# Attention and a feed-forward block on one core: the bias sums in four row groups, the first two pairs' bias by products of their own, and the order of loads and weights

## The chip, the core and the metric

The kernel runs on one core of a Trainium2 chip. The core has a matrix engine (TensorE, PE in the profile), a vector engine (VectorE, DVE), an activation engine (ScalarE, ACT), a general engine (GpSimd, POOL) and an engine that here only issues transfers (SyncE, SP). Each works through its own list of instructions in program order and waits on semaphores where it needs another engine's result. ScalarE, GpSimd and SyncE each have a queue for DMA transfers; an issue that has to wait holds up everything behind it on the same engine. The metric is the time of one execution on the device in microseconds, the median over runs.

## The reference

Eight batches of eight heads, 576 positions, head size 64. With `cum` the running sum of `max(s, 0)` along the positions of one head:

```python
scores = scale * np.matmul(q, k.transpose(0, 1, 3, 2))
bias = -(cum[:, :, :, None] - cum[:, :, None, :])
scores = np.where(causal, -1000000000.0, scores + np.minimum(bias, 0.0))
attn = softmax(scores)
x = (attn @ v), heads side by side: 4608 tokens x 512
h = x @ w_in                      # 512 x 2048
g = h * np.clip(h + 3.0, 0.0, 6.0) / 6.0
out = g @ w_out                   # 2048 x 512, float32
```

## The kernel before

**Pairs.** The 64 heads are worked in 32 pairs `p`, four pairs (`PPB`) to a batch. For each pair q and k are loaded (`load_qk`, 288 KB each), cast to f16 (`cast_qk`, a tile `tok`), transposed into a tile `qk` with head size on partitions 0 to 63 (`transpose`, `order`), and v is loaded and cast (`load_v`, `cast_v`). There are three buffers each of raw q/k, raw v, `qk` and `va`, so a load waits for the cast three pairs earlier, and the writing of `qk` waits for the scores three pairs earlier. Pairs 0 to 8 are transposed on TensorE; from pair 9 (`NPE`) on a crossbar DMA does it (`crossbar_qk`, issued by SyncE, tile `jt`), and `spread` copies its result into `qk` on VectorE.

**Scores.** `scores(p, hh, g)` makes one 128x512 bank of scores (keys on partitions): `g == 0` holds the four diagonal blocks, `g` 1 and 2 what lies off the diagonal; `corner` makes the last 64 queries of both heads. ScalarE takes the exponential of each bank. `av` multiplies with v, `norm` divides, `transpose_x` (later `crossbar_x`) puts the result into `xT`.

**Bias.** The bias is a product of four rows in partitions 64 to 67 of `qk`, beside the 64 rows of q and k: the query side holds -c, 1, 1, 1, the key side 1 and c in three f16 pieces whose sum is c exactly enough (c is 8 times the running sum). These rows are made for all 64 heads at once on 64 partitions, one head each, in lines 536 to 551: `spos`, the scan `c8`, and then casts and differences on ScalarE and VectorE into `aug`. `load_aug` then moves one head's rows from `aug` to four partitions of `qk` by DMA, issued by SyncE for pairs 0 to 2 and by GpSimd after.

**Causal mask.** In pairs 0 to 3 a product of `ident2` (twice the identity) and `shut` (0 or -65504) is added to the diagonal blocks. From pair 4 on the diagonal blocks contract over all 128 partitions: partitions 68 to 127 hold a fixed staircase (`set_stair`) and VectorE takes the minimum with `masks` after the exponential.

**Feed-forward.** `m1` makes one 128x512 piece of h from four products over `xT` and a slice of `w_in`, then ScalarE and VectorE make `gT`; `m2` multiplies with `w_out`. `group()` picks the next m1 or m2 that is ready when the program is written; before the first m2 only every second call does work, so pairs 4 to 6 hold four m1 each. A block's m1 may begin once its batch has gone through attention, so the first m1 stands in pair 4. The weights come in four pieces of `w_in` and eight of `w_out`, issued by GpSimd (`next_weights`) in the pair loop: none in pair 0, one a pair in 1 to 4, two in 5 and 6, three in 7.

**Order.** The order on each engine is written out by hand; no planner moves it. The loop (line 579) first gives GpSimd and SyncE the work for pairs ahead (aug rows for pair p+2, cast of q and k for p+2, v for p+1, weights, loads for p+3 or p+4), and then the pair's own products, with `get(0)` and `get(1)` where a coming pair's q and k are transposed. Ahead of the loop stand the loads of pairs 0 to 2, the fills, the bias rows and the transposes of pairs 0 and 1.

Of the kernel before, what the change touches and what calls it, by code (L numbers as in the profile page):

```python
# [18 lines left out]
def kernel(  # L19
# [27 lines left out]
    VW = 66  # L47

# [6 lines left out]
    masks_dram = nc.inline_tensor(  # L55
        np.concatenate([tri] * 4 + [tri4] * 2, axis=1).astype(np.float16), name="masks"
# [40 lines left out]
    aug = keep("aug", [NHEADS, 4, 2, SEQ], F16)  # L97
# [41 lines left out]
    def load_aug(p, engs):  # L139
        for hh, eng in enumerate(engs):  # L140
            g = 2 * p + hh
            eng.dma_start(  # L142
                out=qks[p % NQK][64:68, hh, :, 64 * hh : 64 * hh + SEQ],
                in_=aug[g : g + 1, :, :, :],
            )
# [136 lines left out]

    def scores(p, hh, g):
# [3 lines left out]
        by_product = p < PPB  # L287
        if g == 0:
            rows = slice(0, 68 if by_product else 128)
            if by_product:  # L290
                mm(S, lhsT=ident2, rhs=shut[:, 0:512], start=True, stop=False)
            for j in range(4):
# [8 lines left out]
        else:  # L301
            for j in ((0, 3) if g == 1 else (1, 2)):
# [7 lines left out]
                    stop=(c != 0),  # L310
                )
        c = slice(512 * g, 512 * (g + 1))
# [6 lines left out]
    def corner(p):  # L319
        S = s_bank([128, 2, 64], "Sc")  # L320
        by_product = p < PPB
# [9 lines left out]
        for hh in range(2):  # L331
            qT, kT = qk_of(p, hh)
            mm(  # L333
# [86 lines left out]
    def m1(n, ft):  # L420
        if ft == 0:
            gTs[n] = work.tile([128, NFT, 512], F16, tag="gT", bufs=2, name="gT")
        ph = psum.tile([128, 512], F32, tag="ph", bufs=2, name="ph")
        for kc in range(NKC):
# [6 lines left out]
            )  # L431
        tr = work.tile([128, 512], F32, tag="tr", bufs=3, name="tr")
# [64 lines left out]
    s_all = work.tile([NHEADS, SEQ], F32, tag="s_all", bufs=1)  # L497
    nc.sync.dma_start(out=s_all, in_=s.rearrange("b h t -> (b h) t"))
    nc.scalar.dma_start(out=stair_sb, in_=stair_dram.ap())
    load_qk(0, 0, nc.sync)  # L500
    load_qk(0, 1, nc.scalar)
    nc.scalar.dma_start(out=ident, in_=ident_dram.ap())
    nc.scalar.dma_start(out=masks, in_=masks_dram.ap())
# [3 lines left out]
    load_v(0, nc.sync)  # L507

# [9 lines left out]
    fill(nc.gpsimd, aug[:, 0, 1, :], 1.0)  # L518
    fill(nc.gpsimd, aug[:, 1:4, 0, :], 1.0)
    for i in range(NQK):  # L520
        init_va(i, nc.gpsimd)
    ones = work.tile([NHEADS, SEQ], F32, tag="ones", bufs=1)
    nc.vector.memset(ones, 1.0)
    nc.vector.memset(bias3, 3.0)
    for i in range(NQK):
        for hh in range(2):
            r = SEQ + 64 * hh
            nc.vector.memset(qks[i][0:64, hh, :, r : r + 64], 0.0)
    for t in Ps:
        fill(nc.vector, t[:, 1536:1664], 1.0)  # L530
    for t in PCs:
        fill(nc.vector, t[:, 128:192], 1.0)
    set_stair(0, nc.gpsimd.tensor_copy)
    set_stair(1, nc.gpsimd.tensor_copy)

    spos = work.tile([NHEADS, SEQ], F32, tag="spos", bufs=1)
    nc.vector.tensor_scalar(
        out=spos, in0=s_all, scalar1=0.0, scalar2=8.0, op0=ALU.max, op1=ALU.mult
    )
    c8 = work.tile([NHEADS, SEQ], F32, tag="c8", bufs=1)  # L540
    nc.vector.tensor_tensor_scan(
        out=c8, data0=ones, data1=spos, initial=0.0, op0=ALU.mult, op1=ALU.add
    )
    nc.scalar.mul(out=aug[:, 0, 0, :], in_=c8, mul=-1.0)
    nc.vector.tensor_copy(out=aug[:, 1, 1, :], in_=c8)
    r1 = work.tile([NHEADS, SEQ], F32, tag="s_all", bufs=1, name="r1")
    nc.vector.tensor_tensor(out=r1, in0=c8, in1=aug[:, 1, 1, :], op=ALU.subtract)
    nc.vector.tensor_copy(out=aug[:, 2, 1, :], in_=r1)
    nc.vector.tensor_tensor(
        out=aug[:, 3, 1, :], in0=r1, in1=aug[:, 2, 1, :], op=ALU.subtract  # L550
    )

    cast_qk(0, nc.scalar.copy, nc.scalar.copy)
    load_aug(0, (nc.sync, nc.sync))
    for i in range(2):
        load_qk(2, i, nc.sync)
# [151 lines left out]
```

## Time and profile before

| | |
|---|---|
| median of 13 runs | 374.43 us (372.36 to 377.52) |
| profiled execution | 374.06 us |
| its span | 372.3 us |
| TensorE busy | 347.0 us (93%) |
| VectorE busy | 242.8 us (65%) |
| ScalarE busy | 219.5 us (59%) |
| GpSimd busy | 118.7 us (32%) |

A line of the timeline or of the POOL order has its start in us, its length, the engine, the line of the kernel, the operation, what is written and read, the shape, how many were merged, and in brackets the idle time before it and what ended it. A line of the waits names the waiting engine and line, what it waited for, and the sum in us, the number of times and the longest. In the stretches each engine's busy time stands with its number of instructions (PE, PEld, DVE, ACT, POOL), then the granted TensorE clock, the DMA share and GB/s. A matmul's length is until its result is there; back to back they follow each other faster than that. Pair `p`'s first product in the trace is at 15.28 us for p = 0, 21.53, 27.32 and 30.76 for 1 to 3, 38.48 for 4, 46.42, 53.96, 61.20, 71.00 and 80.72 for 5 to 9.

### The profile page before, as it was taken

What the parts mean: (1) busy time and instruction counts of PE and PEld (TensorE: products, weight loads), DVE (VectorE), ACT (ScalarE), POOL (GpSimd) and SP (SyncE); (2) the same over time, 40 slices, a digit from 0 to 9 for tenths busy, and PEclk for the clock granted to TensorE, in tenths of its full rate; (3) what the DMA queues carried; (4) which work ended last, traced back from release to release, by engine and by line L of the source; (5) the groups of instructions that cost most, each with busy time, mean ns of one, the idle gap of its engine ahead of it and who ended that gap; (6) DMA issues with size and microseconds to landing.
All of it is one profiled execution on the core that took longest, in us unless ns stands there. A gap on an engine that the chain in (4) does not pass through costs nothing.

```text
span 372.3 us, 7613 instructions
## 1 busy us (share of the span) xinstructions
PE 347.0 (93%) x2845; PEld 193.3 (52%) x2845; DVE 242.8 (65%) x541; ACT 219.5 (59%) x384; POOL 118.7 (32%) x214
## 2 busy tenths in 40 slices
PE   1597999879999899999999999999999999999995
PEld 0376666445555455555555555555555444444442
DVE  6655799567778977777777777777775554544531
ACT  3456798646667566666666666666666334344310
POOL 9373949543335233333333333333300000000000
PEclk9999799989999999999999999999999999999999
DMA  9579999999989999899989999998311010010012
GB/s 188 110 148 223 225 238 218 202 206 215 209 178 176 218 185 172 183 178 178 178 152 204 178 171 185 177 180 150 81 48 46 30 55 30 30 56 29 30 56 85
DMA packets 158189, 54.01 MB, mean 145 GB/s; under 512 B 146928, under 2 KB 153248, under 8 KB 158152
## 3 DMA queue, kind: packets, MB, share of 16 engines
q1 hardware_dynamic: 150408, 48.23, 65.7%
q0 software_dynamic: 6144, 4.74, 7.7%
q10 hardware_dynamic: 1600, 0.56, 0.7%
q8 instruction: 22, 0.36, 0.4%
q14 instruction: 15, 0.12, 0.1%
HBM read 37.11 MB, written 9.44 MB: 125 GB/s over the span
## 4 chain that ended last, share of the span: by engine, by line
PE 76%; DMA 10%; SPq 5%; POOL 4%; DVE 2%; issue 2%; ACT 0%; POOLq 0%
PE po L445 32%; PE ph L425 29%; PE O L362 6%; PE S L305 5%; DMA raw<-in_q_dram 5%; DMA vraw<-in_v_dram 3%; PE S L294 3%; DMA jt<-tok 2%; SPq L130 1%; SPq L134 1%; SPq L119 1%; POOL tok L194 1%; POOL tok L190 1%; POOL qk L142 1%; DVE qk L226 1%
## 5 line engine op out<-in xcount | busy, mean ns | idle before, releaser
L434 DVE SCALAR_TENSOR_TENSOR gT<-tr,ph 128x512 f16<-128x512 f32 x144 | 98.6, 685 | 89.8 <-ACT tr L433 89.1
L425 PE MATMUL ph<-xT,w_in_sb 128*128 128x512 f16 x576 | 149.3, 382 | 0.3 <-DVE gT L434 0.3
L433 ACT ACTIVATE tr<-ph,bias 128x512 f32<-128x512 f32 x144 | 99.0, 687 | 82.8 <-PE ph L425 71.8
L445 PE MATMUL po<-w_out_sb,gT 128*128 128x512 f16 x576 | 145.6, 379 | 1.3 <-DVE x L385 1.3
L313 ACT ACTIVATE P<-S 128x512 f16<-128x512 f32 x192 | 112.0, 595 | 41.9 <-PE S L294 20.9
L445 PEld LDWEIGHTS <-gT 128*128 128x128 f16 x576 | 50.3, 98 | 47.6 <-DVE x L385 1.4
L425 PEld LDWEIGHTS <-w_in_sb 128*128 128x128 f16 x576 | 51.5, 98 | 44.6 <-issue 1.5
L142 POOL DMA_DIRECT2D qk<-aug x58 | 34.0, 587 | 122.1 <-PE Sc L333 58.3
L362 PE MATMUL O<-va,P 128*128 128x65 f16 x896 | 49.6, 197 | 4.3 <-POOL va L202 2.2
L305 PE MATMUL S<-qk 68*128 68x448 f16 (+3 forms) x256 | 50.8, 284 | 0.2 <-ACT P L313 0.2
L362 PEld LDWEIGHTS <-P 128*128 128x128 f16 x896 | 41.3, 100 | 17.6 <-DVE x L385 2.4
L305 PEld LDWEIGHTS <-qk 68*128 68x128 f16 x256 | 24.6, 102 | 24.7 <-issue 1.4
L194 POOL CAST tok<-raw 128x576 f16<-128x576 f32 x51 | 32.7, 673 | 8.2 <-DMA raw<-in_q_dram 6.5
L226 DVE COPY qk<-jt 64x768 f16<-64x768 f16 x92 | 31.7, 344 | 3.5 <-DMA jt<-tok 2.1
L385 DVE TENSOR_TENSOR x<-O,rl 128x320 f16<-128x320 f32 x64 | 31.5, 492 | 2.2
L454 DVE TENSOR_SCALAR ob<-po 128x512 f32<-128x512 f32 x36 | 24.6, 682 | 9.5 <-PE po L445 9.5
L294 PEld LDWEIGHTS <-qk 128*128 128x128 f16 (+1 forms) x256 | 20.3, 101 | 16.2 <-issue 2.6
L315 DVE TENSOR_TENSOR P<-P,masks_sb 128x512 f16<-128x512 f16 x56 | 24.7, 440 | 4.8 <-ACT P L313 4.8
L294 PE MATMUL S<-qk 128*128 128x128 f16 (+1 forms) x256 | 26.1, 226 | 1.5 <-DVE qk L226 0.9
L202 POOL CAST va<-vraw 128x512 f16<-128x512 f32 x32 | 19.9, 623 | 4.4 <-DMA vraw<-in_v_dram 2.5
L240 PE MATMUL pt<-ident,tok 128*128 128x128 f16 (+1 forms) x40 | 6.1, 288 | 12.1 <-ACT tok L194 8.2
L384 DVE RECIPROCAL rl<-O 128x5 f32<-128x5 f32 x64 | 12.1, 189 | 6.5 <-PE O L362 6.5
(49 smaller groups left out, 151.5 us busy)
## 6 DMA issues: line engine op xcount, KB each, us to landing
raw<-in_q_dram SPq DMA_DIRECT2D x32, 288.0 KB, 6.3
out_dram<-ob SPq DMA_DIRECT2D x36, 256.0 KB, 2.2
raw<-in_k_dram SPq DMA_DIRECT2D x31, 288.0 KB, 7.2
vraw<-in_v_dram SPq DMA_DIRECT2D x64, 128.0 KB, 4.4
w_in_sb<-in_moe_w_in_dram POOLq DMA_DIRECT2D x4, 512.0 KB, 9.5
w_out_sb<-in_moe_w_out_dram POOLq DMA_DIRECT2D x8, 256.0 KB, 6.6
vraw<-in_v_dram SPq DMA_DIRECT2D x32, 32.0 KB, 3.4
qk<-aug POOLq DMA_DIRECT2D x58, 9.0 KB, 3.5
```

Source lines behind the costliest of these rows:

```text
L142: eng.dma_start(out=qks[p % NQK][64:68, hh, :, 64 * hh : 64 * hh + SEQ], in_=aug[g : g + 1, :, :, :],)
L194: eng(out=tok[:, 9 * D * i : 9 * D * (i + 1)], in_=raws[p % NRAW][:, 9 * D * i : 9 * D * (i + 1)],)
L226: copies[par](out=qk[0:64, :, i, 128 * par : 128 * par + 256 * n].rearrange("p h (s two c) -> p h s two c", two=2, c=128)[:, :, :, 0, :], ...
L294: mm(S[:, c], lhsT=kT[rows, c], rhs=qT[rows, c], start=(j == 0 and not by_product), stop=(j == 3),)
L305: mm(S[:, c : c + w], lhsT=kT[0:68, 128 * j : 128 * (j + 1)], rhs=qT[0:68, 128 * (j + 1) : SEQ], start=(c == 0), stop=(c != 0),)
L313: nc.scalar.activation(out=pt[:, c], in_=S, func=AF.Exp, scale=0.125)
L362: mm(o[:, i, :], lhsT=lhsT, rhs=va[:, hh, j, 0:65], **kw)
L385: nc.vector.tensor_tensor(out=X[p][:, :, hh, :], in0=o[:, :, 0:64], in1=rl.to_broadcast([128, 5, 64]), op=ALU.mult,)
L425: mm(ph, lhsT=w_in_sb[:, kc, ft * 128 : (ft + 1) * 128], rhs=xT[:, kc, n * 512 : (n + 1) * 512], start=(kc == 0), stop=(kc == NKC - 1),)
L433: nc.scalar.activation(out=tr, in_=ph, func=AF.Relu, bias=bias3[:, 0:1])
L434: nc.vector.scalar_tensor_tensor(out=gTs[n][:, ft, :], in0=tr, scalar=6.0, in1=ph, op0=ALU.min, op1=ALU.mult)
L445: mm(po, lhsT=gTs[n][:, ft, t4 * 128 : (t4 + 1) * 128], rhs=w_out_sb[:, ft, :], start=(ft == 0), stop=(ft == NFT - 1),)
```

## The change

**Bias rows.** s is loaded for 32 heads at a time, four copies on 128 partitions, so each head has four partitions (32 apart). `rows_of[n]` holds the query side and the key side of all four rows. It is made by `cum1` to `cum6`: for heads 0 to 31 ahead of the loop, mostly on VectorE, and for heads 32 to 63 in pairs 6 to 11, mostly on GpSimd with the scan on VectorE. `load_aug` reads `rows_of`.

**Pairs 0 and 1.** They have no `load_aug`. Rows 64 to 67 of their `qk` are zero, and their bias is added by products over all 128 partitions of `rows_of` with `picked`, a copy of the query side in which `sel` leaves only one head's four partitions: nine more products a head.

**Queues.** SyncE issues no `load_aug` any more; pair 2's goes to GpSimd. Pair 0 to 2's loads go out ahead of everything that waits for a result; `load_v(p + 3)` moves to the top of the loop. ScalarE's queue has two pieces of s, k of pair 0, ident, shut, and stair last. Pair 1's casts go to GpSimd.

**Masks and stairs.** `shut` is loaded instead of `masks`; GpSimd makes `masks` in pair 4. Pair 4 now uses the product with `shut` too. The staircases are set on GpSimd in pairs 4 and 5 (six copies), none ahead of the loop. Pair 5's `load_aug` moves from pair 3 to pair 4.

**Order.** Each of pairs 0 to 7 transposes the next pair, in pairs 0 to 3 after the second bank and before head 1. Weights: one piece in pairs 2 and 3, three in 4, four in 5, three in 6. In pair 4 two m1 begin with three of their four products (`m1_begin`), ahead of the last head's `av` and after the second bank.

```diff
-    aug = keep("aug", [NHEADS, 4, 2, SEQ], F16)
+    rows_of = keep("rows_of", [128, 2, 640], F16, 2)
+    sel = keep("sel", [128, 4], F32)
+    picked = keep("picked", [128, 4, SEQ], F16)
...
+    def by_rows(p, hh, out, keys, queries):
+        mm(
+            out,
+            lhsT=rows_of[0][:, 1, keys],
+            rhs=picked[:, 2 * p + hh, queries],
+            start=False,
+            stop=False,
+        )
...
-        by_product = p < PPB
+        by_product = p <= PPB
...
+            if p < NROW:
+                for j in range(4):
+                    c = slice(128 * j, 128 * (j + 1))
+                    by_rows(p, hh, S[:, c], c, c)
...
+            if p < NROW:
+                for j in ((0, 3) if g == 1 else (1, 2)):
+                    c = OFF[j] - 512 * g
+                    w = 448 - 128 * j
+                    mm(
+                        S[:, c : c + w],
+                        lhsT=rows_of[0][:, 1, 128 * j : 128 * (j + 1)],
+                        rhs=picked[:, 2 * p + hh, 128 * (j + 1) : SEQ],
+                        start=False,
+                        stop=(c != 0),
+                    )
...
+    def m1_begin(n, ft, kcs):
+        if (n, ft) not in phs:
+            ph = psum.tile([128, 512], F32, tag="ph", bufs=2, name="ph")
+            phs[n, ft] = [ph, 0]
+        ph, have = phs[n, ft]
+        for kc in range(have, kcs):
...
-    s_all = work.tile([NHEADS, SEQ], F32, tag="s_all", bufs=1)
-    nc.sync.dma_start(out=s_all, in_=s.rearrange("b h t -> (b h) t"))
+    def load_s(n, engs):
+        C[n] = work.tile([128, SEQ], F32, tag="s_all", bufs=1, name="s_all")
+        heads = s.rearrange("b h t -> (b h) t")[32 * n : 32 * (n + 1), :]
+        for r, eng in enumerate(engs):
+            eng.dma_start(out=C[n][32 * r : 32 * (r + 1)], in_=heads)
+
+    load_s(0, (nc.sync, nc.scalar, nc.sync, nc.scalar))
+    load_qk(0, 1, nc.scalar)
+    load_qk(0, 0, nc.sync)
+    nc.scalar.dma_start(out=ident, in_=ident_dram.ap())
+    nc.scalar.dma_start(out=shut, in_=shut_dram.ap())
     nc.scalar.dma_start(out=stair_sb, in_=stair_dram.ap())
...
+    for i in range(2):
+        load_qk(2, i, nc.sync)
+    load_v(1, nc.sync)
...
+    fill(nc.gpsimd, rows_of[0][:, 0, :], 1.0)
+    fill(nc.gpsimd, rows_of[0][:, 1, SEQ:640], 0.0)
+    for i in range(NROW):
+        fill(nc.gpsimd, qks[i][64:68, :, :, :], 0.0)
...
-    set_stair(0, nc.gpsimd.tensor_copy)
-    set_stair(1, nc.gpsimd.tensor_copy)
...
+    nc.vector.tensor_reduce(
+        out=sel,
+        in_=ident.rearrange("p (r g) -> p g r", r=4)[:, 0:4, :],
+        axis=mybir.AxisListType.X,
+        op=ALU.add,
+    )
+    nc.vector.tensor_scalar_mul(out=ident2, in0=ident, scalar1=2.0)
...
+    V = nc.vector
+    cum1(0, V)
+    cum2(0)
     cast_qk(0, nc.scalar.copy, nc.scalar.copy)
-    load_aug(0, (nc.sync, nc.sync))
...
+    nc.scalar.copy(out=rows_of[0][0:32, 0, 0:SEQ], in_=C["c"][0:32])
     for i in range(2):
         load_qk(3, i, nc.sync)
     load_v(2, nc.sync)
+    cum3(0, V)
+    cum4(0, V)
+    cum5(0, V)
+    cum6(0, V)
+    pick(0)
+    transpose(0, 0, (nc.scalar.copy, nc.vector.tensor_copy))
+    transpose(0, 1, (nc.scalar.copy, nc.scalar.copy))
+    for g in range(1, 2 * NROW):
+        pick(g)
+    cast_qk(1, nc.gpsimd.tensor_copy, nc.gpsimd.tensor_copy)
+    for i in range(2):
+        load_qk(4, i, nc.sync)
     cast_v(0)
+    load_aug(2, nc.gpsimd)
...
+    weights_in = {2: 1, 3: 1, 4: 3, 5: 4}
     for p in range(NP):
         nxt = p + 1 < NP
-        if 0 < p < NP - 2:
-            load_aug(p + 2, (nc.gpsimd, nc.gpsimd))
-        c = 3 if p == 0 else p + 2
-        if p != 1 and c < NP:
+        if p + 3 < NP:
+            load_v(p + 3, nc.sync)
+        if p == 4:
+            set_stair(2, nc.gpsimd.tensor_copy)
+            load_aug(5, nc.gpsimd)
+            set_stair(0, nc.gpsimd.tensor_copy)
+            nc.gpsimd.tensor_scalar(
+                out=masks, in0=shut, scalar1=65504.0, scalar2=None, op0=ALU.add
+            )
+        if p == 5:
+            set_stair(1, nc.gpsimd.tensor_copy)
+        if 0 < p < NP - 2 and p != 3:
+            load_aug(p + 2, nc.gpsimd)
+        c = p + 2
+        if p and c < NP:
             cast_qk(c, nc.gpsimd.tensor_copy, nc.gpsimd.tensor_copy)
...
-        next_weights(0 if p < 1 else 1 if p < 5 else 2 if p < 7 else 3)
+        next_weights(weights_in.get(p, 3 if p > 2 else 0))
...
+        if p == 6:
+            load_s(1, (nc.sync,) * 4)
+            fill(nc.gpsimd, rows_of[1][:, 0, :], 1.0)
+        if p == 8:
+            cum1(1, nc.gpsimd)
+        if p == 9:
+            cum2(1)
+            nc.gpsimd.tensor_copy(out=rows_of[1][0:32, 0, 0:SEQ], in_=C["c"][0:32])
+        if p == 10:
+            cum3(1, nc.gpsimd)
+            cum4(1, nc.gpsimd)
+        if p == 11:
+            cum5(1, nc.gpsimd)
+            cum6(1, nc.gpsimd)
...
             scores(p, 0, 1)
+            get(0)
             scores(p, 0, 2)
...
+            get(1)
             scores(p, 1, 0)
             scores(p, 1, 1)
-            get(0)
...
         if p == PPB:
+            early[0] = False
+            scores(p, 0, 0)
             av(p - 1, 1, 0)
+            m1_begin(0, 0, NKC - 1)
             av(p - 1, 1, 1)
             norm(p - 1, 1)
-            scores(p, 0, 0)
             scores(p, 0, 1)
+            m1_begin(0, 1, NKC - 1)
             transpose_x(p - 1)
-            early[0] = False
+            group()
+            group()
             scores(p, 0, 2)
             get(0)
-            group()
-            group()
```

## The prediction

> **What bounds it now.** First the page, part 2: TensorE is busy in tenths 9 nearly throughout, except in the first nine slices of 9.3 us. So the end is set by TensorE, and only gaps and slow clock near the start can be won.
>
> ```profile
> PE   1597999879999899999999999999999999999995
> ...
> PEclk9999799989999999999999999999999999999999
> ```
>
> Then the stretches of 5 us:
>
> ```profile
> 10.00:15.00 5.00, 1.29 (x9) 0.82 (x9) 4.89 (x10) 1.24 (x2) 1.88 (x3) 1.00 0.03 6
> 15.00:20.00 5.00, 4.94 (x35) 3.23 (x35) 0.99 (x3) 4.16 (x8) 1.76 (x3) 1.00 0.97 188
> ...
> 35.00:40.00 5.00, 4.14 (x50) 3.58 (x50) 1.93 (x6) 2.54 (x5) 4.99 (x9) 0.54 1.18 218
> ...
> 75.00:80.00 5.00, 3.57 (x27) 2.31 (x28) 2.81 (x9) 0.89 (x3) 0.66 (x2) 0.66 1.47 217
> ```
>
> From 10 to 15 us nothing loads (6 GB/s) and VectorE works 4.89 of 5 us; at 35 and 75 us the granted clock drops. The waits, Sync's queue first, name the causes: the bias rows hold Sync 3.7 us; v is cast late; the crossbar's jt lands late.
>
> ```profile
> SPq L142 <- DVE aug L549: 3.7, 1, 3.7
> ```
> ```profile
> PE O L362 <- POOL va L202: 2.2, 1, 2.2
> ...
> DVE qk L226 <- DMA jt<-tok: 2.1, 1, 2.1
> ```
>
> The timeline gives the prices: S by ident2 and shut took 0.61 us at 15.28 and 0.39 at 27.32.
>
> ```profile
> 2.98 6.36 POOL L511 COPY qk<-stair_sb 64x1280 f16<-64x1280 f16 x4
> ...
> 8.26 1.68 DVE L547 TENSOR_TENSOR r<-c,aug 64x576 f32<-64x576 f32 x1
> ...
> 15.28 0.61 PE L291 MATMUL S<-shut,ident 128*128 128x512 f16 x1
> ...
> 15.69 0.63 PE L294 MATMUL S<-qk 68*128 68x128 f16 x4
> ```
> ```profile
> 27.32 0.39 PE L291 MATMUL S<-shut,ident 128*128 128x512 f16 x1
> ...
> 27.55 0.39 PE L294 MATMUL S<-qk 68*128 68x128 f16 x4
> ```
> ```profile
> 26.81 1.16 POOL L142 DMA_DIRECT2D qk<-aug  x2
> 30.19 0.82 POOL L190 CAST tok<-raw 96x768 f16<-96x768 f32 x1 [2.22 <-DMA raw<-in_q_dram]
> 34.43 0.82 POOL L190 CAST tok<-raw 96x768 f16<-96x768 f32 x1 [3.42 <-DMA raw<-in_k_dram]
> 35.20 0.61 POOL L202 CAST va<-vraw 128x512 f16<-128x512 f32 x1
> ```
>
> **Bias chain.** The sum c was ready at 6.86 (4.57 + 2.29). Now VectorE first takes sel and ident2 from ident, which stands behind two s pieces (148 KB) and k on ScalarE's queue. Masks, next behind ident, landed 5.8 us after issue, at 8.2; ident at about 6.2, plus 1.0 for what is put ahead of it (an estimate, at half of the 225 GB/s of that stretch): 7.2. Then 0.3 for sel and ident2, spos 0.6, scan 2.3 and gaps 0.2: c at 10.6, 3.7 us later. The casts and differences after it took 6.97 to 12.05, 5.1 us, because each ran into a GpSimd copy.
>
> **A rule against the row.** L547 began at 8.26; the last stair copy ended at 9.34; 9.34 + 0.6 is its end, 9.94. The Trainium skill ("SBUF — State Buffer", Who interferes with whom) says why: VectorE and GpSimd share a port pair held for a whole instruction, the other waits. The stairs leave the start, but casts of pair 1 on GpSimd (0.67 each) begin at 11.4, inside the new chain. By undisturbed rows (0.45 + 0.6 + 0.4 + 0.6 + pick 0.35) the rows stand at 13.2; by the rule, one cast between each two steps, at 14.9. I take 14.4, nearer the rule, since L548 and L549 at 9.98 and 10.86 alternated with casts just so.
>
> At nothing, with their cover: GpSimd's fills of rows_of and of qk rows 64 to 68 (0.82 for 864 elements in L174, so 1.45 for each 1536) end by 6, its next work waits for c until 11; without that cover, 3 us. ScalarE's two more issues (0.35 to 0.69 each) and its table load of 1.28 end near 5.3, before q has landed (before, cast at 7.48). The stair load, now last, is first read in pair 4. Picks 1 to 3 (0.35 each) lie under head 0's slow products.
>
> **Products.** Each head of pairs 0 and 1 gains nine products of 1600 columns, 3200 a pair. From L294, (0.63 - 0.31)/3 for 128 columns slow, 0.058 fast: 2.7 us a pair slow, 1.45 fast. Before, S began at 15.28, pair 0 took 6.25 (to 21.53), pair 1 5.79 (to 27.32), pair 2 3.44. After: pair 0 slow is 6.25 + 2.7 = 8.95; pair 1 fast is 3.44 + ten transposes 0.65 + 1.45 = 5.5. Transposing pair 1 inside pair 0 replaces pair 2's transposes, so nothing else changes there.
>
> **The clock, rule and row.** The skill ("TensorE: Matmul & The Clock Gate", Part 1) gives half clock until one busy window of about 3.4 us, free-running. The stretches fit such windows: 0.54 and 0.78 after 35 us mean slow from about 35.4 to 42.2, two windows; 0.66 means one. But from 15.28 TensorE was dense and still took 0.62 for S at 24.27: the PEclk row shows nothing of it. By the rule alone pair 0 would be fast from about 18, by the row only from 24.7. What tells the windows apart is a guess of mine: counting columns at the slow 0.83 ns, those that stayed slow spent 60 to 63% on products other than transposes, those that freed it 65 to 91%. The added products raise pair 0 to about 73%. I take one window earlier, 21.3. Pair 0: 14.4 + 6.9 + 1.05 = 22.4; pair 1 ends at 27.9, its last score 0.55 earlier as before: T = 27.35, against 26.78.
>
> **GpSimd after T.** Its aug load for pair 4 must wait for that last score. Queued behind it, in order, by rows: aug 0.6, two casts 1.65, v 0.9, w_in 0.78; next pair casts 1.65, v 0.9, w_in 0.78; then pair 4: stair 3.2 (two of 1.6), aug 1.2, stair 3.2, masks 0.8, aug 1.2, casts 1.65, v 0.9, three weights 2.3; then pair 5: stair 3.2, aug 1.2, casts 1.65. Sum 27.8, so pair 7's tok is ready at 55.1. Masks has no row; 0.8 is half a stair copy for half its elements, ends 0.3 (VectorE's L565) and 1.5. TensorE used tok 7 at 54.19: it is 0.95 late, and TensorE waits for it: pairs 2 and 3 take 4.0 each (3.44 and five or six transposes twice), so pair 4 begins at 35.9; pairs 4 and 5 take 7.4 each (before, pair 5 began at 46.42, 6 at 53.96, 7 at 61.20) and some 2 for w_in below, so it would ask at about 53.5.
>
> ```profile
> 54.19 0.42 PE L246 MATMUL pt<-ident,tok 96*128 96x96 f16 x6
> ```
>
> So most of what the loads win is handed to this queue. w_in 0, issued at T + 3.15 = 30.5 instead of 26.03, lands in 7.2 to 9.8 (before's least and most): 37.7 to 40.3, asked for at 36.6. That wait of 1 to 3.7 stays under GpSimd's. The other three pieces are wanted one pair each later.
>
> **Loads.** Sync no longer waits for aug, so the 5 idle us carry 1.0 MB and q, k, v of pairs 2 to 4 come about 4 us earlier; that alone removes the 2.2 us wait at 33.4 and the slow 35.4 to 42.2, worth 5 if nothing replaced it. The queue above does. Sync moves past load_v, four s loads (4 x 0.5 us issue, under pairs of 7 us) and no aug.
>
> **jt.** Pair 9's crossbar was issued at 67.29, landed in 7.76; VectorE's spread held norm and TensorE (74.3 to 76.4), then one slow window: about 3 us. After: the cast ends at T + 27.8 + 12.7 = 67.9, and fewer loads stand before it. Median landing over all jt is 6.0: 73.9, wanted near 73 in a program 0.95 late. I take 2.3 of the 3; ends 0 and 3.5.
>
> **The rest.** Pair 4 by product: 1152 columns, 0.5 us, hidden under GpSimd's wait; without that cover, +0.5. It saves three VectorE minima. The products begun early fill a gap, no more work. Pairs 8 to 11 get the second sum: a 2.3 us scan on VectorE, and GpSimd steps of about 0.7 to 1.5 (estimates from its casts, doubled for two inputs). VectorE has 20 to 30% free there; L315 took 1.36 instead of 0.42 at 116.99 beside a cast. I add 0.4, ends 0 and 1.5.
>
> **Sum.** +0.95 - 2.3 + 0.4 = -0.95. Profiled execution: 374.06 with a span of 372.3, 1.76 around it; so 373.1. The median shown is 374.43, 0.37 above, so 373.5.
>
> **Rivals.** *Early clock* (0.30): the gate opens at 17.9. Pair 0 ends at 20.7, T is 25.65, pair 7's tok 0.75 early; jt saves the whole 3.5, 0.2 lost later: 370.4. For it: the products' density; against: 9 us of slow, dense work before.
>
> *GpSimd's queue is the bound, slower* (0.26): the gate opens at 24.7 as before. Then T is 29.0, tok 7 is 2.6 late, jt is late with it and saves nothing, 0.5 later: 377.5. It decides from T above 28.3, where lateness 1.9 plus 0.4 eats the 2.3. For it: 9.6 us of stair copies that before lay at 2.98 to 9.34, under the loads; against: from 26 to 53 us GpSimd lost 10.7 us to waits for DMA (2.22 and 3.42 of them above), which the earlier loads take away.
>
> *Hidden anyway* (0.10): the start does not move since ident and port waits put the rows at 15.3 and loads are again held by casts: 374.4.
>
> **Numbers.** Sum case 0.34, rest as given. The measurement tells about 0.5% from nothing, 372.6 to 376.3. Faster: the early clock's 0.30 and 0.09 of the sum's case; slower: 0.26 and 0.02; same 0.33. Range 369.2 to 378.2, from the early clock less 1.2 (weights and jt at best) to the queue's case plus 0.7; the sum's own range, 371.5 to 375.6, from the ends of jt and masks.
>
> **What would show it.** First S near 14.4; S products of 0.39 from about 21; loads busy from 10 to 15; GpSimd without a gap from 27 to 58, and TensorE waiting for tok in pairs 5 or 6; no wait for jt near 74. Wrong if the rows stand before 13 or after 16, if GpSimd's stair copies take other than 1.6, or if VectorE's port waits stall pairs 8 to 11.

## The result: 1.3% slower, where 0.2% faster was forecast

The changed kernel took 379.20 us, the median of 11 runs (377.39 to 379.85), against 374.51 us for the kernel before, measured beside it. The ratio is 1.0126, with a 95% interval of 1.0102 to 1.0149. The forecast was 373.5 us, 0.2% faster, with a range up to 378.2, so both the sign and the range were missed. The profiled execution after took 378.55 us with a span of 376.7; before, 374.06 with 372.3. The difference that has to be found is 4.4 us of span.

The page of the changed kernel, its row of TensorE and its row of the granted clock:

```profile
PE   1598888649999899999999999999999999999995
...
PEclk9999999959999999999999999999999999999999
```

Each digit is 9.4 us. The slow clock of the fifth slice is gone, as the loads were to do, but there is a hole of 4 in the ninth slice, at 75 to 85 us, and the clock there is 0.5. In stretches of 5 us (columns as before: PE, PEld, DVE, ACT, POOL busy, clock, DMA share, GB/s):

```profile
10.00:15.00 5.00, 1.19 (x10) 1.06 (x10) 4.80 (x10) 2.63 (x4) 4.44 (x7) 1.00 1.35 217
...
35.00:40.00 5.00, 3.67 (x45) 2.26 (x43) 1.65 (x5) 2.06 (x4) 4.89 (x6) 1.00 1.18 231
40.00:45.00 5.00, 4.55 (x62) 2.97 (x59) 4.63 (x8) 4.87 (x11) 5.00 (x8) 1.00 0.63 158
45.00:50.00 5.00, 4.44 (x54) 2.82 (x51) 4.92 (x11) 4.79 (x10) 4.95 (x7) 1.00 0.95 134
...
75.00:80.00 5.00, 0.00 (x0) 0.00 (x0) 0.75 (x4) 0.00 (x0) 3.35 (x4) 0.50 0.91 185
```

From 10 to 15 us the DMA engines now carry 217 GB/s instead of 6. From 40 to 50 us they carry 158 and 134, where the kernel before had 235:

```profile
40.00:50.00 10.00, 10.00 (x102) 6.17 (x101) 8.87 (x16) 8.30 (x17) 6.70 (x12) 0.89 1.20 235
```

From 75 to 80 us TensorE of the changed kernel does nothing at all. The waits say what for, first all engines, then Sync's own:

```profile
PE O L394 <- DVE x L417: 8.6, 2, 8.3
...
DVE qk L232 <- DMA jt<-tok: 8.3, 1, 8.3
```
```profile
SPq L134 <- POOL va L209: 11.5, 3, 8.0
```

VectorE's spread of pair 9 (L232) waits 8.3 us for the crossbar's result jt, norm (L417) stands behind it, and TensorE behind norm. Before, the same wait was 2.1. On Sync one load of v waited 8.0 us for a v cast of GpSimd. Its timeline shows what came of that:

```profile
35.78 0.44 SPq L118 DMA_DIRECT2D raw<-in_k_dram  x1
44.23 0.94 SPq L134 DMA_DIRECT2D vraw<-in_v_dram  x2
...
47.82 5.91 SPq L123 DMA_DIRECT2D raw<-in_k_dram  x1
53.83 8.21 SPq L134 DMA_DIRECT2D vraw<-in_v_dram  x2
...
66.51 7.06 SPq L545 DMA_DIRECT2D s_all<-in_s_dram  x4
73.68 1.22 SPq L134 DMA_DIRECT2D vraw<-in_v_dram  x2
...
75.72 1.36 SPq L274 DMA_TRANSPOSE jt<-tok  x1
```

Sync issues nothing from 36.2 to 44.2 us: `load_v(8)`, moved to the top of the loop body of pair 5, waits for `cast_v(5)`, and q and k of pairs 8 and 9 stand behind it. From 48 on single lines of this list take 5 to 8 us, where the kernel before had 3.7 at most:

```profile
54.39 3.71 SPq L130 DMA_DIRECT2D vraw<-in_v_dram  x2
...
67.29 2.43 SPq L268 DMA_TRANSPOSE jt<-tok  x1
```

The crossbar of pair 9 goes out at 75.72 instead of 67.29, though its cast was done at 67.1. Up to 47.8 us Sync is not behind the kernel before: there q of pair 8 was issued at 49.29, here at 45.92. The hold uses up the lead that the early loads had won, and the changed kernel falls behind in the full stretch after it. GpSimd's timeline shows why the v cast came so late:

```profile
32.97 2.45 POOL L563 COPY qk<-stair_sb 64x1280 f16<-64x1280 f16 x2
35.36 1.19 POOL L146 DMA_DIRECT2D qk<-rows_of  x2
36.55 2.45 POOL L563 COPY qk<-stair_sb 64x1280 f16<-64x1280 f16 x2
39.10 1.82 POOL L669 TENSOR_SCALAR masks_sb<-shut 128x640 f16<-128x640 f16 x1
40.89 1.17 POOL L146 DMA_DIRECT2D qk<-rows_of  x2
42.05 1.61 POOL L196 CAST tok<-raw 96x768 f16<-96x768 f32 x2
43.59 0.62 POOL L208 CAST va<-vraw 128x512 f16<-128x512 f32 x1
44.15 0.29 POOL L209 CAST va<-vraw 64x128 f16<-64x128 f32 x1
```

In pair 4 the stairs, the masks, two moves of bias rows and the q/k casts, some 11 us, stand ahead of the cast that Sync waits for.

How the 4.4 us add up is read from the first product of each pair:

| pair | before | after | after minus before |
|---|---|---|---|
| 4 | 38.48 | 34.61 | -3.87 |
| 5 | 46.42 | 44.06 | -2.36 |
| 7 | 61.20 | 58.66 | -2.54 |
| 8 | 71.00 | 68.98 | -2.02 |
| 9 | 80.72 | 84.75 | +4.03 |

The changed program is 3.9 us ahead at pair 4 and still 2.0 at pair 8. Between pair 8 and pair 9 it loses 6.0, the growth of TensorE's wait there from 2.1 to 8.3. From pair 9 to the end it loses another 0.4.

### The profile page after: what moved, and what is told of

Read it like the earlier page. It is cut to its first block, busy times and chain, and to the rows that moved or that the text cites. A ratio compares the mean times of both kernels' runs of the same rounds, so it can differ in the third digit from the quotient of the medians.

```text
span 376.7 us, 7742 instructions
## 1 busy us (share of the span) xinstructions
PE 345.2 (92%) x2884; PEld 191.8 (51%) x2884; DVE 243.8 (65%) x541; ACT 219.3 (58%) x383; POOL 134.2 (36%) x231
## 2 busy tenths in 40 slices
DMA packets 158485, 54.41 MB, mean 144 GB/s; under 512 B 147072, under 2 KB 153344, under 8 KB 158448
## 4 chain that ended last, share of the span: by engine, by line
PE 77%; DVE 7%; DMA 6%; POOL 3%; issue 2%; ACT 2%; ACTq 0%; SPq 0%; POOLq 0%; DVEq 0%
PE po L487 31%; PE ph L460 30%; PE O L394 6%; PE S L324 6%; PE S L313 3%; DMA raw<-in_q_dram 2%; DMA w_in_sb<-in_moe_w_in_dram 2%; DMA ident<-ident_f 2%; DVE gT L476 1%; DVE qk L232 1%; DMA jt<-tok 1%; ACT tr L475 1%; POOL tok L196 1%; DVE x L417 1%; ACT P L343 1%
## 5 line engine op out<-in xcount | busy, mean ns | idle before, releaser
L146 POOL DMA_DIRECT2D qk<-rows_of x60 | 35.4, 590 | 122.4 <-PE Sc L365 52.4
L394 PE MATMUL O<-va,P 128*128 128x65 f16 x896 | 48.2, 193 | 8.6 <-DVE x L417 8.6
L394 PEld LDWEIGHTS <-P 128*128 128x128 f16 x896 | 39.8, 97 | 22.0 <-DVE x L417 9.2
L324 PE MATMUL S<-qk 68*128 68x448 f16 (+3 forms) x256 | 49.8, 276 | 0.2 <-ACT P L343 0.2
L232 DVE COPY qk<-jt 64x768 f16<-64x768 f16 x92 | 34.1, 371 | 9.6 <-DMA jt<-tok 8.3
L200 POOL CAST tok<-raw 128x576 f16<-128x576 f32 x52 | 33.9, 684 | 4.6 <-DMA raw<-in_q_dram 4.1
L417 DVE TENSOR_TENSOR x<-O,rl 128x320 f16<-128x320 f32 x64 | 31.5, 492 | 2.2
L313 PEld LDWEIGHTS <-qk 128*128 128x128 f16 (+1 forms) x256 | 19.5, 98 | 15.7 <-issue 2.4
L313 PE MATMUL S<-qk 128*128 128x128 f16 (+1 forms) x256 | 25.1, 220 | 1.5 <-DVE qk L232 0.9
```

The source lines that it names most:

```text
L146: eng.dma_start(out=qks[p % NQK][64:68, hh, :, 64 * hh : 64 * hh + SEQ], in_=rows_of[g // 32].rearrange("(r g) i t -> g r i t", g=32)[g % ...
L200: eng(out=tok[:, 9 * D * i : 9 * D * (i + 1)], in_=raws[p % NRAW][:, 9 * D * i : 9 * D * (i + 1)],)
L232: copies[par](out=qk[0:64, :, i, 128 * par : 128 * par + 256 * n].rearrange("p h (s two c) -> p h s two c", two=2, c=128)[:, :, :, 0, :], ...
L313: mm(S[:, c], lhsT=kT[rows, c], rhs=qT[rows, c], start=(j == 0 and not by_product), stop=(j == 3),)
L324: mm(S[:, c : c + w], lhsT=kT[0:68, 128 * j : 128 * (j + 1)], rhs=qT[0:68, 128 * (j + 1) : SEQ], start=(c == 0), stop=(c != 0 and p >= NROW),)
L394: mm(o[:, i, :], lhsT=lhsT, rhs=va[:, hh, j, 0:65], **kw)
```

## The experiments

The question was what makes pair 9's crossbar late. At first there were three theories. S: the four loads of s, which stand on Sync ahead of it and took 7.06 us there. D: the DMA engines are full from 50 to 72 us and hold up whatever Sync issues next. G: GpSimd's stairs keep casts and loads back.

Two things hold for all the runs below. Each version was measured beside the kernel before, whose median was then 374.6 to 375.2 us; so versions are compared by their ratios, and 0.1% is 0.37 us. And each trace is of one execution, which need not be a typical one: with the v loads back it took 374.87 us (median 373.09), with four v tiles 375.87 (373.83), with the v loads back and the sum first 373.53 (370.28, and no run was slower).

**The s loads behind the crossbar.**

```diff
-        if p == 6:
+        if p == 7:
             load_s(1, (nc.sync,) * 4)
+        if p == 6:
             fill(nc.gpsimd, rows_of[1][:, 0, :], 1.0)
```

> The changed kernel with the four loads of the second half of s moved from pair 6 to pair 7, behind the crossbar of pair 9 in Sync's queue. Theory S (Sync's order: the four s loads, 7.06 us in the queue from 66.51, hold the crossbar): v of pair 10 starts at 66.5, the crossbar is issued near 69 to 71 instead of 75.72, lands in 3.5 to 5, TensorE's wait of 8.3 us before 80.54 shrinks to 3 or less: 5 us less, about 374. Rival D (the DMA engines are full from 50 to 72 us and hold whatever comes next on Sync): v of pair 10 takes the 5 us in the queue instead, the crossbar is issued at 73 or later, 2.5 us less at most: 376.7 or more.

Measured: 378.13 us, ratio 1.0113 (1.0058 to 1.0167). The time that the s loads had taken on Sync went to the v load behind them; the crossbar went out at 73.29 and TensorE waited 6.1 us. Sync's timeline of this run:

```profile
66.23 5.96 SPq L134 DMA_DIRECT2D vraw<-in_v_dram  x2
...
73.29 1.41 SPq L274 DMA_TRANSPOSE jt<-tok  x1
```

What fills Sync is not s itself but that nothing can be issued quickly then. The four runs do not tell this version from the changed kernel (1.0126). S falls.

**The v loads back behind the q and k loads.**

```diff
-        if p + 3 < NP:
-            load_v(p + 3, nc.sync)
         if p == 4:
...
                     load_qk(m, i, nc.sync)
+        if p + 3 < NP:
+            load_v(p + 3, nc.sync)
         if p == 6:
```

> The changed kernel with the v loads for pair p+3 back behind the crossbar and the q and k loads of the loop, as before the change; the s loads stay in pair 6 ahead of the crossbar. Theory S: the crossbar of pair 9 passes the v loads of pair 10, which stood 2.0 us in Sync's queue, and still waits for the s loads: issue near 73.7, 2 us less, about 377.2. Rival D: the order of v is nothing to a full DMA; 379 and the crossbar's issue near 75.

Measured: 373.09 us, ratio 0.9935 (0.9899 to 0.9971). By the ratios this one edit takes 1.9% (some 7 us) off the changed kernel and makes it faster than the kernel before. That was more than any theory had said. Sync's timeline:

```profile
38.55 0.81 SPq L118 DMA_DIRECT2D raw<-in_q_dram  x1
39.41 0.45 SPq L118 DMA_DIRECT2D raw<-in_k_dram  x1
...
66.06 2.44 SPq L545 DMA_DIRECT2D s_all<-in_s_dram  x4
68.60 1.92 SPq L274 DMA_TRANSPOSE jt<-tok  x1
```

q and k of pair 8 go out at 38.55 instead of 45.92 us, the DMA engines carry 201 GB/s from 40 to 50 us instead of 146, and the crossbar is out 7.1 us earlier; TensorE still waits 3.9 us behind norm at pair 9. A new theory, V, follows: `load_v` at the top of the body waits for a v cast that GpSimd reaches late, and holds q and k of the coming pairs behind it; the DMA engines run half empty meanwhile, are full later, and cannot catch up before pair 9's crossbar.

**Fewer weights early.**

```diff
-    weights_in = {2: 1, 3: 1, 4: 3, 5: 4}
+    weights_in = {2: 1, 3: 1, 4: 2, 5: 2, 6: 2, 7: 3, 8: 1}
```

> The changed kernel with the weight pieces of pairs 4 to 8 spread as 2, 2, 2, 3, 1 instead of 3, 4, 3 in pairs 4 to 6. Sync's order stays. Theory S: Sync's queue still meets the four s loads ahead of the crossbar; 377.5 to 379.5. Rival D: with 0.5 MB of weights less in the DMA queues between 52 and 68 us the s loads take about 3 us instead of 7 in Sync's queue, the crossbar is issued 4 us earlier, 375; and pair 8's aug rows wait less on GpSimd (58.95).

From pair 4 on these are as many pieces, pair by pair, as the kernel before had issued. Measured: 376.87 us, ratio 1.0070 (1.0036 to 1.0105), 0.6% under the changed kernel. The crossbar went out at 70.40. Part of the gain came back as a wait of TensorE for w_out (2.1 us), and its wait behind norm at pair 9 was 2.9. So the earlier weights are a part of the loss and not the larger one, and what is put off is soon wanted.

**The stairs in earlier pairs.**

```diff
+    set_stair(2, nc.gpsimd.tensor_copy)
     load_aug(2, nc.gpsimd)
...
+        if p in (1, 2):
+            set_stair(p - 1, nc.gpsimd.tensor_copy)
         if p == 4:
-            set_stair(2, nc.gpsimd.tensor_copy)
             load_aug(5, nc.gpsimd)
-            set_stair(0, nc.gpsimd.tensor_copy)
...
-        if p == 5:
-            set_stair(1, nc.gpsimd.tensor_copy)
```

> The changed kernel with the six staircase copies taken out of GpSimd's pairs 4 and 5 and set ahead of the bias loads of pairs 2, 3 and 4, where GpSimd waited 0.45, 2.09 and 2.30 us for TensorE. Theory G (GpSimd's 7.3 us of stairs keep casts back, so loads pause at 39 to 45 us and pile up at 50 to 72): pair 4's work on GpSimd starts 2.5 us later than 32.97 but pair 6's and 7's casts 2.5 and 5 us earlier, loads between 40 and 50 above 146 GB/s, the crossbar earlier by 2 or more: 376 to 377. Theory S alone: pair 4's weights come later, nothing else: 379 to 380.

Measured: 379.05 us, ratio 1.0120 (1.0067 to 1.0173). The stairs now delayed the first piece of w_in, for which TensorE waited 6.0 us at 41.2, and Sync still stood until 45.3. The v cast that Sync waits for still ended at 45.5, now because the q and k casts ahead of it waited 2.4 and 0.8 us for their loads. Moving GpSimd's work to another pair only moved the wait; this run neither confirms G nor clears GpSimd.

**Four raw v tiles: the wait taken away, the order kept.** This is the sharpest test of V. The load of v for pair 8 goes into a tile that was free long before.

```diff
-    vraws = keep("vraw", [128, 2, 5, D], F32, NRAW)
+    vraws = keep("vraw", [128, 2, 5, D], F32, 4)
...
-        vraw = vraws[p % NRAW]
+        vraw = vraws[p % 4]
...
-    ones = work.tile([128, SEQ], F32, tag="ones", bufs=1)
-    nc.vector.memset(ones, 1.0)
+    ones = work.tile([128, SEQ], F16, tag="ones", bufs=1)
+    fill(nc.vector, ones, 1.0)
```

> The changed kernel with four raw v tiles instead of three (to make room, the scan's ones are 16-bit), all orders left as they are: load_v of pair 8 now waits for the v cast of pair 4 instead of pair 5's, which is long done. Theory V (that wait, standing ahead of the next pair's q and k loads on Sync, leaves the DMA engines idle at 40-45 us and full to 72): the 8.0 us wait of L134 is gone, q and k of pair 8 are issued at about 38-39 us instead of 45.9, jt at about 68-69, and the time is within 1 us of the run with the v loads put back: 373 us or so, ratio 0.992 to 0.997. Theory D (the order of the bytes in the full stretch decides, the wait is only a bystander): v still goes ahead of q and k, jt stays at 75 or so, 378 to 379 us. Theory G (GpSimd's casts are what is late): unchanged, 378 to 379.

Measured: 373.83 us, ratio 0.9989 (0.9962 to 1.0015): 1.4% (5 us) under the changed kernel, with v still ahead of q and k. Sync's timeline:

```profile
39.83 0.63 SPq L118 DMA_DIRECT2D raw<-in_q_dram  x1
40.51 0.45 SPq L118 DMA_DIRECT2D raw<-in_k_dram  x1
...
67.56 1.36 SPq L274 DMA_TRANSPOSE jt<-tok  x1
```

The crossbar goes out at 67.56, and nothing waits for jt any more. V stands, and D and G in the form that they were given fall. The 16-bit ones, which made room for the fourth tile, changed nothing at the start: the scan took 1.36 us as before and the first product stood at 13.83 (13.95). The ratio is 0.002 (0.7 us) above the range that V gave. In the profile TensorE waited 3.2 us for w_in 0 at 38.7 instead, and its clock was 0.50 from 39.7 to 49.9; six of the 21 runs, of 372.3 to 373.9 us, had a granted clock of 1.00 throughout, so this does not happen in every execution.

**The same edit alone in the kernel before.**

```diff
         nxt = p + 1 < NP
+        if p + 3 < NP:
+            load_v(p + 3, nc.sync)
...
                     load_qk(m, i, nc.sync)
-        if p + 3 < NP:
-            load_v(p + 3, nc.sync)
```

> The kernel before with that one edit alone: load_v(p + 3) at the top of the loop body. Its GpSimd has no stairs and no masks to set in pairs 4 and 5, so the v cast that load_v waits for is early. Theory V (two edits are needed together: the v loads ahead AND the late v cast): within 0.4% of before, jt of pair 9 issued at 67 to 69. A rival (v ahead of q and k is costly by itself): 3 to 6 us slower than before, jt at 72 or later.

Measured: 376.89 us, ratio 1.0064 (1.0032 to 1.0096), crossbar at 69.50. That lies between the two expectations. `load_v` waits here too, but 3.5 us at most instead of 8.0; no stairs and masks stand ahead of the v casts. So the order is bad by itself (0.6%, 2.4 us), and the longer hold of the changed kernel goes with a larger loss (1.4 to 1.9% by the two runs above). My statement that both are needed was too strong.

**Both Sync edits.** The v loads back and the s loads behind the crossbar, the two diffs above together.

> The changed kernel with the v loads back behind the q and k loads, and the four s loads of the second half one pair later, behind pair 9's crossbar. With the v loads back the four s loads still took 2.44 us of Sync just ahead of the crossbar (issued at 68.60, its jt awaited for 3.9 us). Theory V+D: jt is issued at about 66.2, its wait falls from 3.9 to about 1.5 us, and the time is 371 (ratio 0.987 to 0.991). If what follows the crossbar takes the pressure instead, as it did when only the s loads were moved: no better than with the v loads back alone, 373.

Measured: 376.26 us, ratio 1.0034 (1.0014 to 1.0054). The crossbar went out at 66.16 and nobody waited for jt, as expected, and yet the time is 1% worse than with the v loads alone (1.0034 against 0.9935). In its profile TensorE waited 2.9 us for w_in 0 and 2.3 us at 69.25, each with a slow clock after it. The first of the two cannot come from the edit: up to pair 6 this program is the same as with the v loads alone, where that wait was 1.7 us. It is a difference between executions. What makes the median worse stays open. An edit that removes the longest wait need not remove its time.

**Half of w_out not loaded.** The changed kernel with the hold on Sync left in. It leaves out half of w_out, 2.1 MB to read; in the MB of the profile, which the GB/s count, that is 1.05 (54.41 against 53.36). The 9 to 10 us of the expectation below are therefore twice too many.

```diff
-                fn(c)
+                if fn is load_w_out and c >= 4:
+                    fill(nc.gpsimd, w_out_sb[:, 2 * c : 2 * (c + 1), :], 1.0)
+                else:
+                    fn(c)
```

> The changed kernel with chunks 4 to 7 of w_out not loaded but filled with ones by GpSimd in their place (so its second feed-forward product is not the reference's): 2.1 MB less for the DMA engines, which at the 0.21 to 0.24 MB/us of the full stretch is 9 to 10 us of it; v loads ahead of q and k as in the changed kernel, with their 8 us wait. Theory V with bytes (the hold costs because the DMA engines are full from 50 to 72 us and cannot catch up): with the bytes gone they catch up, jt of pair 9 is issued at 67 to 69 instead of 75.7, its wait of 8.3 us and the slow clock after it are gone, 369 to 372 us. Theory V without bytes (the late order on Sync alone): the s loads stay short, but q and k of pairs 9 and 10 and so jt stay late, 376 or more.

Measured: 373.51 us, ratio 0.9954 (0.9929 to 0.9979). The s loads took 3.47 us instead of 7.06, the crossbar went out at 71.42, and TensorE waited 3.7 us. That is 1.7% (6 us) off the changed kernel, though neither expectation hit its number: k and v of pair 9 still took 5.6 and 8.3 us to issue, from 49.0 to 63.0, and only what stands behind the missing bytes moved. So it takes two things to lose this time, the hold and the bytes that have to be carried after it: with either gone, the time is about that of the kernel before or less. What the missing bytes would be worth without the hold was not run. These four pieces of w_out are also just what the change asks for earlier: before, eight of the twelve weight pieces were issued by pair 6, three more at 64.17 us in pair 7 and one in pair 8; in the change all twelve are issued by pair 6, the last at 62.13.

**The cumulative sum first on VectorE.** In the change, `sel` and `ident2` stand ahead of the sum and wait for ident until 7.96 us. Here they go behind `cum6`; the v loads are back as well.

```diff
-    nc.vector.tensor_reduce(
+    def selects():
+        nc.vector.tensor_reduce(
...
-    nc.vector.tensor_scalar_mul(out=ident2, in0=ident, scalar1=2.0)
+        nc.vector.tensor_scalar_mul(out=ident2, in0=ident, scalar1=2.0)
...
     cum6(0, V)
+    selects()
     pick(0)
```

> The changed kernel with the v loads back, and the selection tile and doubled identity (both wait for ident, landed at 7.96 us) set behind the cumulative sum and its casts instead of ahead of it on VectorE. The rows' chain then starts when s lands (about 4.3 us): c at 6.5 to 7 instead of 10.0, first score at 11 to 11.5 instead of 14.3. If TensorE's path from there holds the lead: 370 us (ratio 0.984 to 0.990, 3 us under the run with the v loads back alone). If GpSimd's casts or DMA (the loads of pairs 2 to 4 land when they land) set the pace of pairs 2 to 9: the lead is gone by pair 9 and the time is 372 to 373.

Measured: 370.28 us, ratio 0.9885 (0.9853 to 0.9917). This is the fastest version: 1.2% under the kernel before and 2.4% under the change as it was made. VectorE's timeline of this run:

```profile
4.65 1.36 DVE L604 TENSOR_TENSOR_SCAN c<-ones,spos 128x576 f32<-128x576 f32 x1
6.04 0.46 DVE L609 CAST rows_of<-c 128x576 f16<-128x576 f32 x1
6.54 0.76 DVE L615 TENSOR_TENSOR r<-c,rows_of 64x576 f32<-64x576 f32 x1
7.33 0.46 DVE L620 CAST rows_of<-r 64x576 f16<-64x576 f32 x1
7.82 0.76 DVE L624 TENSOR_TENSOR rows_of<-r,rows_of 32x576 f16<-32x576 f32 x1
```

c is ready at 6.0 us instead of 10.0, and the first score stands at 10.5 instead of 14.3. Besides, no step meets a cast of GpSimd any more: L620 and L624 take 0.46 and 0.76, in the changed kernel 0.81 and 1.10.

**The cumulative sum first, the hold left in.** Only the diff just shown.

> The changed kernel with the cumulative sum ahead of the selection tile and doubled identity on VectorE, and nothing else: the v loads stay ahead of q and k, with their wait. First score at 10.5 us instead of 14.3, as in the run that had both edits. If everything behind it moves along (GpSimd's queue hangs on the scores of pairs 0 and 1, Sync's held v load on GpSimd, so both come 3 to 4 us earlier): 375 to 376 us (ratio about 1.003), the same 3 us as with the v loads back. If the bytes decide when pair 9's q and k can come: TensorE only waits longer for jt (11 to 12 us instead of 8.3), 378 to 379 us.

Measured: 378.18 us, ratio 1.0090 (1.0064 to 1.0116). The first score came 3.7 us earlier, and 0.4% (1.3 us) of that reached the end. With the v loads back the same edit was worth 0.5% (1.9 us); the intervals do not tell the two apart. The wait for jt did not grow to 11 or 12 us, as the second expectation had it, but was 7.6: TensorE had lost part of the lead before, with a wait of 2.3 us for w_in 0 at 34.4 and a clock of 0.50 after it. The hold stayed where it was:

```profile
40.00:50.00 10.00, 9.56 (x105) 6.38 (x104) 8.49 (x17) 8.58 (x16) 9.95 (x14) 0.87 0.62 112
```

GpSimd lost its lead in pair 3, where it waited 2.6 us for a transpose of TensorE and 0.6 for k, and gets to the v cast at 43.4 instead of 43.6; Sync is held until 44.0, and 112 GB/s are carried. The crossbar goes out at 74.53.

**Weights earlier.** On top of the fastest version, first only w_in 0 a pair earlier, then all weights by pair 5.

```diff
-    weights_in = {2: 1, 3: 1, 4: 3, 5: 4}
+    weights_in = {1: 1, 2: 1, 3: 1, 4: 3, 5: 4}
```

> The run with the v loads back and the cumulative sum first (370.3 us, 0.9885), and the first chunk of w_in issued one pair earlier (weights_in with 1 at pair 1). There TensorE waited 2.89 us for that chunk at 35.35 us, and its clock was 0.5 for some 6 us after; the waits of 1.72 us and less in all runs left the clock at 1.00. If the chunk is only late in its own turn: it lands before 32.4 us, the wait falls under 1.7 us, the slow stretch after it goes, and the time is 366 to 367 (ratio 0.975 to 0.980). If the bytes of 25 to 75 us are what is short: the wait comes back at w_out or at the crossbar, 369 to 371, as fast as without it.

```diff
-    weights_in = {2: 1, 3: 1, 4: 3, 5: 4}
+    weights_in = {1: 1, 2: 1, 3: 2, 4: 3, 5: 5}
```

> As the run with the first chunk of w_in earlier, and all weights issued by pair 5 (1, 1, 2, 3, 5 from pair 1 on) instead of the last ones at pair 6. If w_out's last chunks are late in their own turn (TensorE waited 2.41 us at 66.7): that wait goes too, 364 to 366. If bytes are short: v and q/k of pairs 7 to 9 are later by as much, a wait at pairs 7 to 9 takes its place, 369 to 372, not better than the run with the first chunk alone.

Measured: 370.74 us, ratio 0.9871 (0.9834 to 0.9907), no different from the version without it; and 374.13 us, ratio 0.9975 (0.9951 to 1.0000). The wait for w_in 0 was gone in both, and another took its place: TensorE waited 2.1 and 7.2 us for the bias rows of pair 5, which GpSimd moves by DMA behind the weights. So the bytes are what is short, and not a place in the order for this chunk, as far as these two runs tell.

**The bytes by 50 us** bring these together. The sum of the GB/s of the five stretches of 10 us, times 10 us, gives what was carried by 50 us:

| version | MB by 50 us | GB/s from 40 to 50 | crossbar of pair 9 out | profiled, us | median, us |
|---|---|---|---|---|---|
| before | 9.18 | 235 | 67.29 | 374.1 | 374.5 |
| changed | 9.53 | 146 | 75.72 | 378.6 | 379.2 |
| changed, sum first | 9.63 | 112 | 74.53 | 377.7 | 378.2 |
| changed, v loads back | 10.36 | 201 | 68.60 | 374.9 | 373.1 |
| changed, v loads back, s late | 10.56 | 203 | 66.16 | 376.2 | 376.3 |
| changed, four v tiles | 10.71 | 228 | 67.56 | 375.9 | 373.8 |
| v loads back, sum first | 10.85 | 211 | 65.41 | 373.5 | 370.3 |

Each row is one profile; the changed kernel with the v loads back and the one with s late as well are the same program up to pair 6, so 0.2 MB is scatter. Taking only the wait away brings 1.18 MB more by 50 us. At the 225 GB/s of the full stretches that is 5.2 us of carrying, an estimate; the median fell by about as much (1.4%, 5 us), the profiled execution by only 2.7. The table separates the versions with the hold from those without, by 0.7 MB and 6 us of the crossbar; it does not put the rest in order: the version with s late has an earlier crossbar than the one with four v tiles and the one with the v loads alone, and a higher median than both. Nor does it hold against the kernel before, which carried least and needs fewer bytes by then.

## Why the prediction was wrong, step by step

**Bias chain: the result right, parts off.** ident landed at 7.96 (7.2 predicted), the scan took 1.36 us instead of 2.29, and c stood at 10.0 instead of 10.6. The first products came at 13.95 and 14.33 against 14.4, so errors on both sides cancelled. I took the scan from the only row there was, and that row lay beside GpSimd's stair copies; without them it is shorter. The four steps after c took 0.46, 0.76, 0.81 and 1.10, the last two beside casts: the rule of the port pair held for those that began beside one, and for them only.

**What I missed in it** is that `sel` and `ident2` needn't wait ahead of the sum. I priced that wait at 3.7 us on c and took it as given; putting the sum first gave 0.4% of the time with the hold and 0.5% without it (1.3 and 1.9 us).

**Products: right.** Pair 1 took 5.5 us as predicted. **Clock: the rival was right.** From TensorE's timeline after:

```profile
13.95 0.59 PE L290 MATMUL S<-picked,rows_of 128*128 128x128 f16 x4 [3.81 <-DVE picked L626]
...
18.39 0.61 PE L306 MATMUL S<-shut,ident 128*128 128x512 f16 x1
18.79 0.43 PE L290 MATMUL S<-picked,rows_of 128*128 128x128 f16 x4
...
26.10 0.38 PE L306 MATMUL S<-shut,ident 128*128 128x512 f16 x1
```

The S product takes 0.61 at 18.39 and 0.38 later; the products are fast from 18.8 on, 4.8 us after dense work began, near the 17.9 of the early-clock rival and not at the 21.3 of the sum. Pair 1's last score stood at 26.05 (T, predicted 27.35).

**GpSimd after T: the sum right, the use of it wrong.** I predicted 27.8 us from T to pair 7's tok and it took 25.9. A stair copy took 1.22 instead of 1.6, the masks 1.82 instead of 0.8. With the earlier T, tok 7 was early, not 0.95 late, and the program ran 2 us ahead where I had it behind; TensorE did wait for a tok once, 1.4 us in pair 7 for pair 8's. But I followed this queue only to TensorE's use of tok. The v casts are in the same list of mine, as "v 0.9", and I did not ask who waits for them.

**Loads: the step that failed.** It says that "Sync moves past load_v, four s loads (4 x 0.5 us issue, under pairs of 7 us) and no aug", and costs that at nothing. Moving `load_v` to the top put it ahead of q and k, and it waits for a v cast; so q and k wait for GpSimd's pair 4. This wait measured 8.0 us, and without it the DMA engines had carried about 1 MB more by 50 us, which they could not make up afterwards. Putting the loads back gave 1.9% (7 us), taking only the wait away 1.4% (5 us). "Fewer loads stand before it", said under jt, overlooked the weights as well, all twelve of which are now issued by 64.3 us, where the kernel before had issued eight by 60.7: without the bytes of the last four the time is 1.7% less, and with the pieces issued as before from pair 4 on 0.6% less. The s loads, costed at 2 us of issue under cover, took 7.06 while the DMA engines were full (212 GB/s from 60 to 70 us, a share of 1.24); alone they were not the cause, since moving them changed the ratio by 0.001.

**jt: its consequence.** "After: the cast ends at T + 27.8 + 12.7 = 67.9, and fewer loads stand before it" had the cast right (67.1) and the loads wrong. The crossbar was issued 8.6 us after its cast, so the forecast of -2.3 became +6.0. Its landing, for which I took 6.0, took only 3.46.

Of the signs of being wrong that I had named, one came: a stair copy took other than 1.6 us. "No wait for jt near 74" was the forecast that failed outright.

**The rest: the number right.** From pair 9 to the end 0.4 us were lost, as I had added. The scan of the second half took 1.49 us instead of 2.3, GpSimd's steps 0.7 to 2.15 instead of up to 1.5; that they make up the 0.4 is not shown.

Put together: predicted 0.95 - 2.3 + 0.4; measured -2.0 + 6.0 + 0.4 = 4.4. The chance of 0.28 for slower lay on a rival that named GpSimd's stairs but let them act through tok and a late T. What the runs show is the way through the v cast, Sync and the DMA engines; setting the stairs elsewhere on GpSimd gained nothing by itself (1.0120).

## What to carry to other kernels

When a load moves ahead of others on a queue, write down what it waits for, where that stands in its own engine's list, and what is queued behind the load; a buffer's release by a slow engine is as much a wait as a result. Where the DMA engines are full for a long stretch, count the bytes carried by a fixed time: here engines a third idle for 10 us came back, over 20 us later, as a wait of 8.3 us at the transfer that was wanted first. And a lead won early must be followed to the end: the sum first moved the first score by 3.7 us and the time by 1.3 to 1.9.

## What the hardware showed that I had not expected

**An issue can take ten times its usual length.** In the changed kernel Sync's issue of a k load by line 123 took 0.37 us at 3.95 and 5.91 at 47.82, two v loads 0.94 at 44.23 and 8.21 at 53.83, a third after it 2.99. These are not waits for a result: the raw v tile of the load at 53.83 had been free since the v cast that ended at 52.73, the tile of s since the bias chain at 13.26, though the profile's list of waits puts part of these times down to later work of GpSimd and VectorE. What holds the issue stays open; the versions without the hold have such issues too (8.25 us for the same v loads in the fastest one). So a price per issue taken from a quiet stretch is worth nothing in a full one.

**TensorE's clock falls after shorter gaps than stated.** The Trainium skill ("TensorE: Matmul & The Clock Gate", Part 1) has the clock halved after an idle window of about 3.4 us. The measurements decide here. In these runs every TensorE gap of 1.96 us or more between 30 and 82 us was followed by a clock of 0.50 within 6 us of its start, or lay in a slow stretch already (1.96, 2.08, 2.11, 2.21, 2.32, 2.34 and longer), and single gaps up to 1.72 left it at 1.00; two gaps of 1.0 and 1.1 close together (the run with fewer weights early) lay in a slow stretch too. The clock came back between 3 and 11 us after work resumed. In stretches of 1 us, the fastest version after a gap of 2.89 us that ended at 35.35 (columns: PE busy, clock, DMA share, GB/s):

```profile
35.00:36.00 1.00, 0.65 (x3) 1.00 1.21 243
36.00:37.00 1.00, 1.00 (x13) 0.87 1.15 260
37.00:38.00 1.00, 1.00 (x7) 0.50 1.15 284
...
43.00:44.00 1.00, 1.00 (x5) 0.71 1.22 212
```

TensorE is busy again at once; the clock falls 1.4 us later, at 36.7, and stays at half until 43.6. At half clock a dense stretch of 3 us loses 1.5 and one of 7 loses 3.5, an estimate from these lengths; a wait of 2 us can so cost twice itself, a wait of 1.7 us only itself.
